# Attention and MLP on one core: PSUM banks named from group 6 on, and q and k of 28 blocks turned by transposing DMA

## The chip, the core and the metric

The kernel runs on one core of one Trainium2 chip. The metric is device time in microseconds (us). A profiled execution, taken by the hardware profiler, is read beside the times.

## The reference

```python
# 8 batches, 8 heads, 576 positions, 64 dimensions of a head; d_model 512, hidden 2048
scores = np.matmul(q, k.transpose(0, 1, 3, 2)) / np.sqrt(64)
rel = pos[:, None] - pos[None, :]
bias = slopes[:, None, None] * -np.abs(rel)          # slopes 2 ** -(h + 1)
scores = np.where((rel >= 0) & (rel < 128), scores + bias, -1e9)
attn = softmax(scores)
x = np.matmul(attn, v).transpose(0, 2, 1, 3).reshape(8, 576, 512)
xn = (x - mean) / np.sqrt(var + 1e-06) * g_ln
out = x + np.maximum(xn @ w_ch1, 0.0) @ w_ch2
```

A query sees itself and the 127 positions before it, so a block of 128 queries needs the keys of its own block and of the one before.

## The kernel before

**Blocks and groups.** The rows are cut into 36 blocks of 128. The batches go in four pairs p; a pair has nine blocks: four of each batch, in turn (`blk` 0, 2, 4, 6 of the first, 1, 3, 5, 7 of the second), and `blk` 8, called `T`, which holds the last 64 rows of both. The list `order` numbers them n = 0 to 35. The MLP works on groups of blocks: groups 0 to 5 have two blocks each (n = 0 to 11), groups 6 to 11 four each (group 6 is n = 12 to 15, group 11 is n = 32 to 35).

**Attention of a block.** q and k arrive with positions along partitions, and the scores need dimensions along partitions. `load_qk` (L213) loads q and k of both batches for 128 positions (index i = `blk // 2`; i = 4 is the tail) into a raw tile, from a pool of four buffers for each of q and k, cast to fp16 on the way by POOL's DMA. It puts two neighbouring positions side by side in a partition, so a piece of a transfer is two rows of 64 numbers. `turn` then does 64 TensorE transposes of 64x64 (L277) into two PSUM banks, and four copies (L296 for q, L297 for k; L302 for the tail), one bank's on VectorE (DVE), the other's on ScalarE (ACT). The queries come out with the even positions first and the odd ones behind; the mask `m_full`, made of exponentials of distances (`decay`, L118), has its columns in the same order, and stores of an output block go out as two DMAs, one of even and one of odd rows. `scores` (`attend`, L381) writes products into one of two score tiles of two PSUM banks each, and ScalarE takes their exponential (L389). `masks` multiplies with the decay on VectorE (L400). `values` multiplies with v, which `load_v` (L223) has loaded (L433), and divides by the sum (L441, L442).

**Layer norm.** `stats` takes mean and variance on VectorE (L530, L531), and two small POOL operations (L485, L488) make `rstd` of them. `normal` centres and scales a block into `xc` (L472) and issues a transposing DMA on SP's queue (L480) that puts it into `xT`, the input of the MLP. Blocks of the first groups are turned by TensorE in place of that.

**MLP.** `mlp1(g)` is the first layer: 16 units of four matmuls into one PSUM bank each (L665), and a ReLU (L681, mostly on ScalarE). For groups 0 to 5 `mlp2` is the second layer (L698) and `finish` (L809) adds x. For groups 6 to 11 `fast_mlp2` does the second layer with seven products of half blocks in place of eight, from sums and differences of quarters of the hidden tile (`combine_hidden`, L733, on VectorE) and of the weights (made once). The products are accumulated in four PSUM banks x, y, z and w, in the order x, y, z, x, z, x, w (L757); after each of them VectorE adds a bank to the output (`add`, L770), and `send` stores two blocks at a time.

**PSUM.** Four of the eight banks are the two score tiles. The others are the pool `ps_mm`, with one tag: each tile that is asked for takes the next of the four in turn, be it for a unit of the first layer, a product of the second, values or a turn. A turn uses the score tiles where its call has `in_sc`, as all those in the loop over the later blocks have.

**Order.** The order of instructions on TensorE, VectorE and ScalarE is written out by hand: `steps` is a list of the attention's steps, and `weave_at(units, places)` goes through the units of a layer and puts the next step behind each unit whose number is in `places`. From group 6 on there is one loop:

```python
for g in range(6, len(GROUPS)):
    weave_at(mlp1(g), 0, 2, 5, 7, 8, 10, 13, 15, also=(1, 4) if g == 6 else ())
    weave_at(fast_mlp2(g), 1, 3, 6, 7, 7, 9, 12, 13)
```

Each block n from 8 on has four steps: a turn of the keys and queries three blocks ahead (if there is one to do); values of n and scores of n + 2; masks of n + 1 and n + 2, and statistics of n; `normal`. Loads are issued on POOL by `load_until`, with each block's values, so far as the list of loads is due (`place`, `AHEAD`). The order on POOL and on SP (loads, small operations, stores, transposing DMAs) is the scheduler's.

Of the kernel before, what the change touches and what calls it, by code (L numbers as in the profile page):

```python
# [11 lines left out]
FP32 = mybir.dt.float32  # L12
# [5 lines left out]
P = 128  # L18
# [4 lines left out]
T = 8  # L23
# [15 lines left out]
def distances():  # L39

    key = np.arange(P)[:, None]
    query = np.arange(P)[None, :]

    def far(rel, ok=True):
        return np.where(ok & (rel >= 0) & (rel < WINDOW), rel, FAR)

    ends = [far(P + query - HALF * b - key, query // HALF == b) for b in range(2)]  # L50
    tail = far(query - key, query // HALF == key // HALF)
    evens_first = np.r_[0:P:2, 1:P:2]
    both = [far(P + query - key), far(query - key)]
    cols = [m[:, evens_first] for m in both] + [*ends, tail]
    return np.concatenate(cols, axis=1).astype(np.float16)
# [3 lines left out]
def kernel(  # L59
# [24 lines left out]
    consts = pool("consts", 1)  # L84
    raw_pool = pool("raw", 4)
    turned_pool = pool("turned", 3)
    probs_pool = pool("probs", 4)
# [13 lines left out]
    dist = consts.tile([P, 5 * P], FP16)  # L101
    nc.sync.dma_start(out=dist, in_=dist_dram.ap())
    iden = consts.tile([P, P], FP16)
# [9 lines left out]

    def decay(m, at):

        n = m.shape[2]
        for h in range(H):
            nc.scalar.activation(  # L118
                out=m[:, h, :],
                in_=dist[:, at * P : at * P + n],  # L120
                func=AF.Exp,
                scale=-(2.0 ** (-8.0 * (h + 1) / H)),
            )

    g_sb = consts.tile([P, NKB], FP32)
# [79 lines left out]
    raw = {}  # L205

    def load_qk(src, tag, p, i):

        n = min(P, S - i * P)
        t = raw_pool.tile([P, H, 2, D], FP16, tag=tag, name=tag)  # L210
        raw[tag, p, i] = t
        for b in range(2):
            nc.gpsimd.dma_start(  # L213
                out=t[b * n // 2 : (b + 1) * n // 2],
                in_=src[2 * p + b, :, i * P : i * P + n, :].rearrange(
                    "h (c r) d -> c h r d", r=2
                ),
            )
# [64 lines left out]
    def turn(p, i, in_sc=False, copies=(nc.vector.tensor_copy, nc.scalar.copy)):  # L283

        ps = [bank(b if in_sc else None) for b in range(2)]
        k = keys_tile("k", p, i)  # L290
        if i < 4:
            q = queries(p, i)
            transposed("q", p, i, [t[:, 0] for t in ps])
            transposed("k", p, i, [t[:, 1] for t in ps])
            for b, copy in enumerate(copies):
                copy(out=q[:, b], in_=ps[b][:, 0])  # L296
                copy(out=k[:, b].rearrange("p h (c r) -> p r h c", r=2), in_=ps[b][:, 1])  # L297
        else:
            q = keys_tile("q", p, i)
            for tag, t, dst, copy in zip("qk", ps, (q, k), copies):  # L300
                transposed(tag, p, i, [t[:, 0]])
                copy(out=dst[:, 0].rearrange("p h (c r) -> p r h c", r=2), in_=t[:, 0])  # L302

# [17 lines left out]
    def turn_first():  # L321
# [12 lines left out]
        nc.vector.tensor_copy(out=g_row, in_=ps_row)  # L334

    weights_of, unmasked, scored = {}, {}, []

# [3 lines left out]
    def seen(p, blk, o, t):  # L341


        both, every = slice(0, 2), slice(0, HALF)
        first, second = slice(0, HALF // 2), slice(HALF // 2, HALF)
        if p == 0 and blk < SEEN:
# [4 lines left out]
        if o == blk:  # L351
            return [(0, both, every), (1, both, second)]
        return [(1, both, every), (0, both, first)]

# [64 lines left out]
    def values(p, blk, hg):  # L419

        if hg == 0:
# [4 lines left out]
            if n < BY_DMA:  # L426
                sums[p, blk] = small.tile([P, 2], FP32, tag="sum", name="sum")
        ps = ps_mm.tile([P, 4, D + 1], FP32, tag="mm", name="ps_pv")
        terms = weights_of[p, blk]
# [189 lines left out]
    steps += [values_steps(5)[0], turn_step(6, True), values_steps(5)[1], scores_step(6)]  # L619
    steps += [x_step(5) + masks_of(6), scores_step(7) + variance_of(4), values_steps(6)[0]]  # L620

    steps += [values_steps(6)[1], x_step(6) + masks_of(7), variance_of(5)]
    steps += [*values_steps(7), x_step(7) + variance_of(6)]
    steps += [turn_step(8) + variance_of(7), scores_step(8) + turn_step(9)]
    steps += [[(scores_tail, 0)] + scores_step(9) + masks_of(8)]


    for n in range(8, count):
        first_half, second_half = values_steps(n)
        steps.append(  # L630
            turn_step(n + 3, True) if n + 3 < count and order[n + 3][1] % 2 == 0 else []
        )
# [23 lines left out]
    def mlp1(g, on_dve=()):  # L656
# [5 lines left out]
        for u, fb in enumerate(turn_about if g >= FAST else range(NFB)):  # L662
            ps = ps_mm.tile([P, 4 * P], FP32, tag="mm", name="ps_m1")
            for kb in range(NKB):
# [70 lines left out]
    def fast_mlp2(g):  # L735
# [13 lines left out]

        banks = {}  # L750

        def product(name, lhs, rhs, first):
            if first:
                banks[name] = ps_mm.tile([P, 2, QD], FP32, tag="mm", name="ps_f")
            for pair in range(pairs):
                for fb in range(QF):
                    nc.tensor.matmul(  # L757
                        banks[name][:, pair, :],
                        lhs[:, fb, pair * P : (pair + 1) * P],
                        rhs[:, fb, :],  # L760
                        start=(first and pair == 0 and fb == 0),
                        stop=(fb == QF - 1),
                        skip_group_check=True,
                    )
                yield DM

        def add(name, i, j, to_x):
            x, o = rows(i)
            cols = slice(j * QD, (j + 1) * QD)
            nc.vector.tensor_tensor(  # L770
                out=o[:, :, cols],
                in0=banks[name][:, 0:pairs, :],
                in1=(x if to_x else o)[:, :, cols],
                op=ALU.add,
            )

        def send(i):
            _, o = rows(i)
            for at in range(pairs):
                store(*members[g][i * pairs + at], o[:, at, :])  # L780

# [19 lines left out]
        add("x", 1, 1, False)  # L801
        yield from product("w", a[1][1], t4, True)
        add("w", 1, 0, False)
        send(1)

# [12 lines left out]

    def store(p, blk, o):
        for b, t0, w, p0 in spans(p, blk):  # L820
            dst, src = out[b, t0 : t0 + w, :], o[p0 : p0 + w, :]
            if blk == T:
                nc.sync.dma_start(out=dst, in_=src)
            else:
                dst = dst.rearrange("(c r) d -> r c d", r=2)
                for r in range(2):
                    nc.sync.dma_start(out=dst[r], in_=src[r * HALF : (r + 1) * HALF])

# [18 lines left out]
    with tc.manual_schedule(engines={engine.PE}):  # L847
        with tc.manual_schedule(engines={engine.Activation, engine.DVE}):
# [13 lines left out]
            weave_at(mlp1(5), 0, 1, 4, 8, 10, 12, also=(3, 6, 9))  # L862
            weave_at(mlp2(5), 0, 1, 2, 4, 6, 7)
            for g in range(6, len(GROUPS)):
                weave_at(
# [34 lines left out]
```

## Time and profile before

| what | value |
|---|---|
| median of three runs | 334.84 us (334.58 to 335.43) |
| profiled execution | 334.56 us, of which span 332.8 us |
| instructions | 10421 |
| matmuls of the first layer, L665 | 116.9 us in 640 |
| matmuls of the second layer, L698 and both groups of L757 | 46.0 in 192, 45.8 in 384, 22.5 in 192 |
| masks L400, adds L770 on VectorE | 688 ns and 684 ns each |
| statistics L530, scaling L472 on VectorE | 685 ns and 412 ns each |
| ReLU L681, exponentials of scores L389 on ScalarE | 497 ns and 1026 ns each |
| DMA packets | 101728, of them 92849 under 512 bytes |
| stores of 128 KB, SP's queue | 72, 2.4 us from issue to landing |
| loads of q, k, v of 128 KB, POOL's queue | 32 each, 5.2, 5.6 and 6.5 us from issue to landing |
| granted TensorE clock, by slices | 0.9 or more of full speed; 0.7 in slice 25 and 0.8 in the last |

An engine's busy time is the sum over its instructions; a matmul's weight load (PEld) overlaps with other matmuls and is counted for itself. A line number is that of the helper that issues an instruction, so the three products x, the two z, y and w all stand at L757, told apart by the tile that they read (`ht`, a quarter of the hidden tile, or `hs`, a sum of such). "Waits" lists what ended the idle time ahead of an instruction. The times of all DMA engines together are given as a share of 16 engines' span, or in a window as a mean busy share.

### The profile page before, as it was taken

To read this page: it belongs to the slowest core of one execution; us is meant where nothing else is said; L and a number is where in the kernel's file an instruction comes from. 1 tells how busy PE (TensorE), PEld (TensorE's weight loads), DVE (VectorE), ACT (ScalarE), POOL (GpSimd) and SP (SyncE) were. 2 spreads that over 40 slices of the span, in tenths; PEclk is the share of its full clock that TensorE was granted. 3 is DMA by queue.
4 is the path that set the end of the run, shared out by engine and by line. 5 is a ranking of instruction groups with operands and counts; after the bars stand their busy time and mean duration, and the time that the engine had idled before them with its cause. 6 is when DMAs were issued, how large, how long until landed. Compare 5 with 4: busy or idle time off the path is not lost.

```text
span 332.8 us, 10421 instructions
## 1 busy us (share of the span) xinstructions
PE 309.3 (93%) x4478; PEld 208.2 (63%) x4478; DVE 234.4 (70%) x555; ACT 184.6 (55%) x320; POOL 114.8 (35%) x188
## 2 busy tenths in 40 slices
PE   8889999998999999999799979999899979999992
PEld 3478556757567575558655866567656854685582
DVE  2879777786777887669775986589758975761462
ACT  6688666676656583684278533763287218405600
POOL 8933677666425652813252541300000000000000
PEclk9999999999999999999999997999999999999998
DMA  9999999999599696996396966351430033015005
GB/s 112 167 207 191 189 152 195 173 140 146 47 145 96 76 157 58 160 66 65 42 164 86 97 65 98 85 43 18 81 81 18 18 80 82 18 23 121 0 2 126
DMA packets 101728, 32.34 MB, mean 97 GB/s; under 512 B 92849, under 2 KB 97073, under 8 KB 101682
## 3 DMA queue, kind: packets, MB, share of 16 engines
q0 software_dynamic: 79872, 18.36, 64.9%
q1 hardware_dynamic: 21810, 13.32, 19.4%
q8 instruction: 35, 0.57, 0.8%
q14 instruction: 11, 0.09, 0.1%
HBM read 36.90 MB, written 9.44 MB: 139 GB/s over the span
## 4 chain that ended last, share of the span: by engine, by line
PE 71%; DVE 10%; ACT 7%; POOL 4%; DMA 4%; issue 2%; DVEq 0%; POOLq 0%; ACTq 0%
PE ps_m L665 31%; PE ps_f L757 21%; PE ps_m L698 9%; ACT probs L389 4%; DMA w<-in_moe_w_ch_dram 4%; PE ps_sc L381 4%; PE ps_pv L433 4%; PE ps_sc L277 2%; DVE probs L400 2%; DVE st L530 2%; POOL vx L223 1%; DVE o L770 1%; POOL q L213 1%; DVE k L297 1%; POOL rstd L488 1%
## 5 line engine op out<-in xcount | busy, mean ns | idle before, releaser
L665 PE MATMUL ps_m<-xT,w1g 128*128 128x512 f16 (+1 forms) x640 | 116.9, 337 | 1.1 <-ACT ht L681 0.8
L681 ACT ACTIVATE ht<-ps_m 128x512 f16<-128x512 f32 (+1 forms) x187 | 89.2, 497 | 39.6 <-PE ps_m L665 36.7
L665 PEld LDWEIGHTS <-w1g 128*128 128x128 f16 x640 | 60.1, 98 | 48.8 <-issue 1.8
L389 ACT ACTIVATE probs<-ps_sc 128x1024 f16<-128x1024 f32 x56 | 54.3, 1026 | 39.7 <-PE ps_sc L381 39.7
L757 PE MATMUL ps_f<-w,ht 128*128 128x256 f16 x384 | 45.8, 279 | 8.7 <-DVE o L770 8.7
L757 PEld LDWEIGHTS <-ht 128*128 128x128 f16 x384 | 37.9, 100 | 14.9 <-issue 9.4
L485 POOL TENSOR_TENSOR rstd<-moments,powers 128x1 f32<-128x1 f32 x28 | 5.4, 192 | 118.6 <-DVE moments L531 118.6
L698 PE MATMUL ps_m<-w,ht 128*128 128x512 f16 x192 | 46.0, 380 | 0.0
L223 POOL DMA_DIRECT2D vx<-in_v_dram x40 | 34.7, 880 | 26.7 <-PE ps_pv L433 12.5
L400 DVE TENSOR_TENSOR probs<-probs,m 128x1024 f16<-128x1024 f16 x56 | 37.4, 688 | 9.1 <-ACT probs L389 8.7
L213 POOL DMA_DIRECT2D q<-in_q_dram x40 | 27.3, 688 | 20.2 <-PE ps_sc L277 12.0
L442 DVE SCALAR_TENSOR_TENSOR x<-ps_pv,rec 128x256 f16<-128x256 f32 x72 | 30.6, 425 | 2.5
L213 POOL DMA_DIRECT2D k<-in_k_dram x40 | 26.9, 686 | 5.9 <-DMA w<-in_moe_w_ch_dram 3.6
L698 PEld LDWEIGHTS <-ht 128*128 128x128 f16 x192 | 17.1, 98 | 17.4
L472 DVE TENSOR_SCALAR xc<-x,moments,rstd 128x512 f16<-128x512 f16 x28 | 11.5, 412 | 19.9 <-POOL rstd L488 19.9
L530 DVE BATCH_NORM_STATS2 st<-x 128x6 f32<-128x512 f16 x36 | 24.6, 685 | 0.0
L296 ACT COPY q<-ps_sc 128x512 f16<-128x512 f16 x15 | 8.8, 586 | 28.0 <-PE ps_sc L277 27.8
L381 PE MATMUL ps_sc<-q,k 64*64 64x128 f16 (+1 forms) x1088 | 20.4, 208 | 3.8 <-ACT probs L389 1.1
L441 DVE RECIPROCAL rec<-ps_pv 128x4 f32<-128x4 f32 x72 | 12.7, 176 | 15.9 <-PE ps_pv L433 15.5
L757 PE MATMUL ps_f<-w,hs 128*128 128x256 f16 x192 | 22.5, 273 | 0.0
L770 DVE TENSOR_TENSOR o<-ps_f,x 128x512 f32<-128x512 f32 x24 | 16.4, 684 | 7.6 <-PE ps_f L757 7.5
L433 PEld LDWEIGHTS <-probs 128*128 128x128 f16 x448 | 18.7, 97 | 4.7 <-DVE probs L400 0.3
(79 smaller groups left out, 345.5 us busy)
## 6 DMA issues: line engine op xcount, KB each, us to landing
out_dram<-o SPq DMA_DIRECT2D x72, 128.0 KB, 2.4
q<-in_q_dram POOLq DMA_DIRECT2D x32, 128.0 KB, 5.2
k<-in_k_dram POOLq DMA_DIRECT2D x32, 128.0 KB, 5.6
vx<-in_v_dram POOLq DMA_DIRECT2D x32, 128.0 KB, 6.5
w<-in_moe_w_ch_dram POOLq DMA_DIRECT2D x8, 512.0 KB, 10.7
q<-in_q_dram POOLq DMA_DIRECT2D x8, 64.0 KB, 4.7
k<-in_k_dram POOLq DMA_DIRECT2D x8, 64.0 KB, 4.5
vx<-in_v_dram POOLq DMA_DIRECT2D x8, 64.0 KB, 5.9
```

What stands on the lines that cost most here:

```text
L213: nc.gpsimd.dma_start(out=t[b * n // 2 : (b + 1) * n // 2], in_=src[2 * p + b, :, i * P : i * P + n, :].rearrange("h (c r) d -> c h r d", ...
L223: nc.gpsimd.dma_start(out=vx[p0 : p0 + n, :, 0:D], in_=v[b, :, t0 : t0 + n, :].rearrange("h p d -> p h d"),)
L381: nc.tensor.matmul(in_halves(ps[cols, j, n, t, :])[:, r, queries], kt[rows, hp, cols], in_halves(qt[rows, b, hp])[:, r, queries], start=Tr ...
L389: nc.scalar.activation(out=dst.rearrange("p (n j) q -> p j n q", j=2), in_=ps.rearrange("p j n t q -> p j n (t q)"), func=AF.Exp, scale=in ...
L400: nc.vector.tensor_tensor(out=dst, in0=dst, in1=mask, op=ALU.mult)
L433: nc.tensor.matmul(ps[:, i, :], pr[:, h, t, :], vext[(p * NSLOT + o) % NV][:, h, :], start=(n == 0), stop=(n == len(terms) - 1),)
L442: nc.vector.scalar_tensor_tensor(out=xs[p, blk][:, hg * 4 * D : (hg + 1) * 4 * D].rearrange("p (h d) -> p h d", h=4), in0=ps[:, :, 0:D], s ...
L530: nc.vector.bn_stats(out=st, in_=xs[order[n]])
L665: nc.tensor.matmul(ps[:, 0:cols], w[:, kb, fb * P : (fb + 1) * P], xT[:, kb, 0:cols], start=(kb == 0), stop=(kb == NKB - 1),)
L681: nc.scalar.activation(out=ht[:, fb, 0:cols], in_=ps[:, 0:cols], func=AF.Relu)
L698: nc.tensor.matmul(sums[at], ht[:, fb, at * P : (at + 1) * P], w2[:, fb, :], start=(fb == 0), stop=(fb == NFB - 1),)
L757: nc.tensor.matmul(banks[name][:, pair, :], lhs[:, fb, pair * P : (pair + 1) * P], rhs[:, fb, :], start=(first and pair == 0 and fb == 0), ...
```

## The change

It has these parts:

- **Loads and turns.** `by_dma(p, i)` is true for all of the pairs 1 to 3 and for the tail of pair 0: blocks 8 to 35. For these, `load_qk` loads positions in natural order, one row of 64 numbers as a piece, and `turn` issues transposing DMAs on SP, two for each of q and k (one for a tail), in place of TensorE's transposes and the copies. A turn issued in this way needs no PSUM. The raw pool goes from four buffers to three, the pool of turned tiles from three to four.
- **Order of queries.** Blocks 8 on have their queries in natural order. `m_full` is computed again in that order once block 7's masks have been made: `in_order` loads the distances anew on SP, and eight exponentials follow on ScalarE in two halves. The range of queries that a key half can see, in `seen`, is then a contiguous half. Rows of these blocks are stored with one DMA, not two.
- **Places.** The turns of blocks 8 and 9 (the tail's tile, and the first of pair 1) are called some steps earlier; that of block 11 is called at n = 8, and the later ones four blocks ahead, not three.
- **Banks.** From group 6 on, the four banks of `ps_mm` are four fixed tiles in a list `ring`. `psum()` takes the first of the list and puts it at its end, for the first layer's units and for values. `fast_mlp2` takes the first for x, the second for y and for z too, and the third for w, and leaves the third and fourth to others meanwhile; afterwards the list is put in a new order.
- **Last group.** There w has a bank for each pair of blocks, so that one block's w is added (256 columns of one block) while the other's runs; the second half of the columns is stored ahead of that, and stores alternate between SP's and ScalarE's queue.

```diff
-    cols = [m[:, evens_first] for m in both] + [*ends, tail]
+    cols = [m[:, evens_first] for m in both] + [*ends, tail] + both
...
-    raw_pool = pool("raw", 4)
-    turned_pool = pool("turned", 3)
+    raw_pool = pool("raw", 3)
+    turned_pool = pool("turned", 4)
...
+    def in_order():
+        nc.sync.dma_start(
+            out=dist[:, 0 : 2 * P], in_=dist_dram.ap()[:, 5 * P : 7 * P]
+        )
...
+    def by_dma(p, i):
+        return p > 0 or i == 4
...
+        if by_dma(p, i):
+            t = raw[tag, p, i] = t.rearrange("p h r d -> p (h r d)").rearrange(
+                "p (b h d) -> p b h d", b=2, h=H
+            )
         for b in range(2):
+            if by_dma(p, i):
+                dst = t[:, b] if i < 4 else t[b * n : (b + 1) * n, 0]
+                nc.gpsimd.dma_start(
+                    out=dst,
+                    in_=src[2 * p + b, :, i * P : i * P + n, :].rearrange(
+                        "h p d -> p h d"
+                    ),
+                )
+                continue
...
+        k = keys_tile("k", p, i)
+        if by_dma(p, i):
+            q = keys_tile("q", p, i)
+            for tag, dst in (("q", q), ("k", k)):
+                src = raw.pop((tag, p, i))
+                for b in range(2 if i < 4 else 1):
+                    nc.sync.dma_start_transpose(
+                        out=dst[:, b], in_=src[:, b].rearrange("p h d -> p (h d)")
+                    )
+            return
...
+    ring = []
+    def psum(name, banks=None):
+        if not ring:
+            return ps_mm.tile([P, DM], FP32, tag="mm", name=name)
+        t = (banks or ring)[0]
+        if banks is None:
+            ring.append(ring.pop(0))
+        return t
...
-            return [(0, both, every), (1, both, second)]
-        return [(1, both, every), (0, both, first)]
+            return [(0, both, every), (1, slice(1, 2), every)]
+        return [(1, both, every), (0, slice(0, 1), every)]
...
-    steps += [turn_step(8) + variance_of(7), scores_step(8) + turn_step(9)]
+    steps += [values_steps(6)[1], x_step(6) + masks_of(7) + [(in_order,)], variance_of(5)]
+    steps += [
+        values_steps(7)[0] + turn_step(9),
+        [(decay, m_full, 0, low)] + values_steps(7)[1],
+        x_step(7) + variance_of(6),
+    ]
+    steps += [[(decay, m_full, 0, high)] + variance_of(7), scores_step(8)]
...
-            turn_step(n + 3, True) if n + 3 < count and order[n + 3][1] % 2 == 0 else []
+            [f for m in ahead  # [n + 4], and [11] at n = 8
+             if m < count and order[m][1] % 2 == 0 for f in turn_step(m)]
...
-        banks = {}
+        x_bank, y_bank, *others = ring
+        use = dict(x=[x_bank] * 2, y=[y_bank] * 2, z=[y_bank] * 2, w=others[:1] * 2)
+        if g == len(GROUPS) - 1:
+            use["w"] = others
+        ring[:] = others
...
-        yield from product("w", a[1][1], t4, True)
-        add("w", 1, 0, False)
-        send(1)
+        if use["w"][0] is use["w"][1]:
+            ring[:] = [others[1], y_bank, x_bank, others[0]]
+            yield from product("w", a[1][1], t4, True)
+            add("w", 1, 0, False)
+            send(1)
+        else:
+            low, high = slice(0, QD), slice(QD, DM)
+            send(1, cols=high, queues=(nc.sync, nc.scalar))
+            for at, _ in enumerate(product("w", a[1][1], t4, True)):
+                add("w", 1, 0, False, slice(at, at + 1))
+                send(1, [at], low, (nc.sync, nc.scalar))
+                yield DM
...
+            if by_dma(p, blk // 2):
+                next(queues).dma_start(out=dst, in_=src)
...
+            ring += [ps_mm.tile([P, DM], FP32, tag="mm", name="ps_r") for _ in range(4)]
             for g in range(6, len(GROUPS)):
```

## The prediction

> **What bounds the kernel now.** I read the page first, then the list of who waited for whom on TensorE, then the timeline, one stretch per stage. The page's shares and the chain that ended last:
>
> ```profile
> PE 309.3 (93%) x4478; PEld 208.2 (63%) x4478; DVE 234.4 (70%) x555; ACT 184.6 (55%) x320; POOL 114.8 (35%) x188
> ...
> q0 software_dynamic: 79872, 18.36, 64.9%
> q1 hardware_dynamic: 21810, 13.32, 19.4%
> ...
> PE 71%; DVE 10%; ACT 7%; POOL 4%; DMA 4%; issue 2%; DVEq 0%; POOLq 0%; ACTq 0%
> ```
>
> TensorE carries the span, so an instruction taken off its queue is worth its issue time, and a wait put into it costs its length. Waits there are few (line waited for: total us, times, longest):
>
> ```profile
> PE ps_f L757 <- DVE o L770: 8.7, 4, 2.2
> ...
> PE ps_sc L277 <- DMA k<-in_k_dram: 1.0, 2, 0.5
> PE ps_sc L381 <- DVE k L297: 0.9, 2, 0.7
> ...
> PE ps_sc L381 <- ACT k L297: 0.3, 2, 0.2
> ```
>
> The largest, 8.7 us, comes once in each of groups 6 to 9. Their second layer (`fast_mlp2`) is the product sequence x, y, z, x, z, x, w; here is group 8 (start us, us, engine, line):
>
> ```profile
> 221.69 3.67 PE L757 MATMUL ps_f<-w,ht 128*128 128x256 f16 x32
> ...
> 225.20 2.78 PE L757 MATMUL ps_f<-w,hs 128*128 128x256 f16 x24
> ...
> 226.09 0.55 POOL L488 TENSOR_TENSOR rstd<-rstd,powers 128x1 f32<-128x1 f32 x1
> ...
> 226.97 0.41 DVE L472 TENSOR_SCALAR xc<-x,moments,rstd 128x512 f16<-128x512 f16 x1
> 227.29 0.68 DVE L770 TENSOR_TENSOR o<-ps_f,o 128x512 f32<-128x512 f32 x1
> ...
> 227.91 0.45 PE L277 MATMUL ps_sc<-iden,q 64*64 64x64 f16 x32
> ...
> 228.55 1.05 PE L757 MATMUL ps_f<-w,hs 128*128 128x256 f16 x8
> ...
> 233.81 0.66 DVE L770 TENSOR_TENSOR o<-ps_f,x 128x512 f32<-128x512 f32 x1
> ...
> 234.52 3.65 PE L757 MATMUL ps_f<-w,ht 128*128 128x256 f16 x32 [2.11 <-DVE o L770]
> ...
> 239.07 5.35 PE L665 MATMUL ps_m<-xT,w1g 128*128 128x512 f16 x24
> ...
> 239.56 0.68 DVE L770 TENSOR_TENSOR o<-ps_f,o 128x512 f32<-128x512 f32 x1
> ```
>
> Line 1 is x and y, line 2 z and half of the second x, 227.91 a turn of q and k, 234.52 the third x and w. The third x waits for the add of the second x (233.81), which stands on VectorE behind two masks and the statistics of a block. The add of y ends at 227.97, 2.8 us after y ended at 225.20; nobody waits for it, since z has a bank of its own. VectorE ran without a gap from 221.2 to then.
>
> **The change, part by part.** Sums are made against the profiled execution: 334.56 us, 332.8 of it span. The median of the three runs is 0.28 higher.
>
> *Turns off TensorE.* From the turn's start to the next matmul is 0.64 us at 227.91 and in every full turn, 0.62 in the half turns of i = 4. Twelve full and four half turns go: 12 x 0.64 + 4 x 0.62 = 10.2 us, half of it (5.1) before group 6 starts at 135.3, half behind. VectorE and ScalarE lose 28 copies each, about 17 and 19 us. With the copies go the waits for k in the list above, 0.9 + 0.3, and one of the two for a k load (0.5; the other is at the start, which stays): 1.7, all early but for the 0.2 us that scores behind a turn wait in the later groups (229.79 to 229.98 in group 8), 0.6 over four.
>
> *Mask again.* `m_full` is computed anew: 8 exponentials of 0.41 us (row L118, 128x256) = 3.3 us of ScalarE near 59 to 65 us, half of it between Relus that come every 0.44 us and take 0.39. The copies it loses there come later, so I charge 0.5 of the 1.6 us (bounds 0 and 1.6). Early sum: -5.1 - 1.7 + 0.5 = -6.3.
>
> *z in y's bank.* The order of instructions and their waits in the changed kernel show the first matmul of z waiting for the add of y, and VectorE's order between is unchanged: statistics, add of x, a combination, xc, add of y. No copy of a turn stood in that stretch, so nothing makes it faster. The price is the end of that add + 0.05 us (as 234.47 to 234.52) less the end of y: group 6 2.6, 7 2.6, 8 2.8, 9 2.7, 10 2.0 (293.91 against 291.98), 11 0.9 (318.90 against 318.02). Sum 13.6. The wait of the third x stays: `add("x", 0, 1)` stands behind the same masks.
>
> *POOL's order.* In the new order a load of q or k stands between the two small operations that make rstd, for blocks 8, 12, 14, 16, 19, 21 and 23 among others; before they always follow at once (225.82 and 226.09). Blocks 19 and 23 matter: their xc stands right before the add of y in groups 6 and 7. Block 19's load waits until a transposing DMA has emptied its raw buffer; those (three in SP's queue, 1.19 us each) wait for scores that end at 152.0, so the third is issued at 154.4 and lands by 157.0 (2.6); the load takes 0.9, rstd 0.6, and xc starts at 158.5, not 157.0. Block 23: 192.4, not 191.1. The stall grows by 1.5 + 1.3 = 2.8. Bounds: 0, if the transposes are earlier, and 5.
>
> *The other banks.* The second unit of the next first layer takes w's bank, and waits for the add at 239.56 to 240.24; it would start at 239.07 + 0.86. That is 0.35 in each of groups 6 to 9, 1.4.
>
> *SP and the loads.* 56 transposes of 1.19 us add 67 us to SP's queue; store issues fall from 72 to 49 on SP and 2 on ACT. xT of block 27, the last of group 9, is issued at 227.4, lands by 230, and is needed at 239.07: 9 us of cover. The 64 loads concerned move twice the packets, 128 bytes each as v's: 0.88 us to issue in place of 0.69, 6.5 us to land in place of 5.2. Loads run 20 to 40 us ahead (k for the turn at 118 left at 75), so I take 0. If that cover went, scores would wait for load, issue and transpose, up to 10 us once.
>
> By the Trainium skill (DMA: Bandwidth & Descriptors, Specifications) transfers under 512 B miss line rate, a rule against this part; 92849 of the page's 101728 packets are already below that, and by the rule loads would come later still, which is the DMA rival below.
>
> *The tail.* Today the last add ends at 327.65, four stores are issued 0.6 us apart, and 3.3 us after the last issue the span ends. Afterwards the last add has half the columns (0.4 us), and one store each on two queues follows: 0.3 + 1.7 = 2.0 saved.
>
> Sum: -6.3 - 5.1 - 0.6 + 13.6 + 2.8 + 1.4 - 2.0 = +3.8, which gives **338.4 us**.
>
> **Rivals.**
> *VectorE comes in time (faster).* If the add of y came on average 2.1 us after y rather than 2.7 (16.4 over six groups), the sum would be zero; at 1.5 it is -3.6 and the time 331, with no stall at all 322. For it: VectorE is 17 us lighter. Against: none of that lies in the stretch.
> *The clock.* After its 2.24 us wait, group 7 ran at half clock for 3.4 us:
>
> ```profile
> 198.92 5.32 PE L757 MATMUL ps_f<-w,ht 128*128 128x256 f16 x32 [2.24 <-DVE o L770]
> ...
> 199.40:202.80 3.40, 3.40 (x21) 2.50 (x19) 1.92 (x4) 0.00 (x0) 0.00 (x0) 0.56 0.37 75
> ```
>
> 32 matmuls took 5.32 us in place of 3.65: 1.7 lost. Waits of 2.11, 2.14 and 2.20 did not trigger it. Now there are five waits of 2 to 4 us more. My sum keeps one such event; three more make 343.5. The Trainium skill (TensorE: Matmul & The Clock Gate, Why this matters for your kernels) puts the limit at gaps of about 3 us, so by it only groups 6 and 7 would add events and the sum be 341.8; the trace's 2.24 is below that limit.
> *DMA becomes the bound.* 28672 more packets (48 loads of 512, 16 of 256) at today's mean (64.9% of 332.8 us over 79872) are 78 us of the engines, and 56 transposes at most 2.3 each (all of q1's share over 28) 129: 85% of the span becomes 147%. But shares overlap: the windows view has 2.18 at 60 to 70 us without a wait. If loads run late, one 10 us wait makes 348.
>
> **Numbers.** A measurement of this kernel tells about 0.3%, 1.0 us, from no change. Forecast (336 to 341) 0.45; clock 0.15 and DMA 0.07, both slower; faster by VectorE 0.2; near balance of the terms, within 0.3%, 0.13. Slower 0.67. The range takes the early and POOL bounds and the clock: 332 to 344.5.
>
> **What would show it.** Right: z's first matmul waits for the add of y, 2 to 4 us, six times; no turn before scores of block 8 on; the 2.1 us waits of the third x remain; groups 6 to 9 take longer, the time up to 135 shrinks by 6. Wrong: z starts within 1 us of y's end, scores wait for a transpose, or the first layer waits for xT.

## The result: 402.7 us in place of 334.7, a ratio of 1.193 (1.180 to 1.207)

The changed kernel takes 402.68 us in the median (397.11 to 404.67), the kernel before 334.71 us beside it. The forecast was 338.4 us and its range ended at 344.5. The ratio is that of the two faster of the four executions, 397.1 and 400.8 us; the other two, the profiled one among them, lie more than 1.5% above the fastest and are left out of it. The profiled execution took 404.52 us, its span is 402.7. Lines have moved: L713 is the first layer (L665 before), L811 and L828 the products and adds of `fast_mlp2` (L757, L770), L229 the load of q and k in natural order, L318 the transposing DMAs of a turn, L509 and L517 `normal` (L472, L480), L522 and L525 rstd (L485, L488), L876 the add in `finish`.

The page of the changed kernel: busy time per engine, two queues, and the shares of the chain that ended last:

```profile
PE 322.8 (80%) x3582; PEld 210.0 (52%) x3582; DVE 220.1 (55%) x528; ACT 172.1 (43%) x300; POOL 125.8 (31%) x188
...
q0 software_dynamic: 108544, 18.36, 66.2%
q1 hardware_dynamic: 52178, 20.60, 28.0%
...
PE 38%; DMA 28%; DVE 13%; POOL 10%; issue 6%; ACT 2%; SPq 1%; POOLq 0%; DVEq 0%; ACTq 0%
```

TensorE has 896 instructions fewer and is busy 13.5 us longer; its mean granted clock is 0.907 of full speed, where it was 0.990 before. It held 71% of the chain before; now it holds 38%, and DMA and POOL together hold as much. So the kernel has another bound in part of its time. Who waits for whom tells which (line waited for: total us, times, longest); first TensorE's waits, then, from the list for all engines, three that were 19.9 us, nothing and nothing before:

```profile
PE ps_r L811 <- DVE o L828: 28.5, 10, 6.1
PE ps_pv L470 <- DVE ht L721: 13.9, 1, 13.9
PE ps_m L713 <- DVE x L479: 7.8, 2, 5.5
PE ps_m L713 <- DVE o L876: 6.7, 3, 3.6
```

```profile
DVE xc L509 <- POOL rstd L525: 77.7, 24, 19.0
...
POOL k L229 <- DMA k<-k: 38.0, 9, 6.7
...
POOL q L229 <- DMA q<-q: 27.9, 10, 6.5
```

TensorE waits for VectorE, VectorE's `xc` waits for POOL's rstd, and POOL's loads of q and k wait for transposing DMAs (`k<-k`, `q<-q`) that have yet to empty a raw buffer. The longest of these waits, in the timeline of all engines (start us, us, engine, line; idle time and its end in brackets):

```profile
82.09 0.18 DVE L568 BATCH_NORM_AGGREGATE moments<-st 128x2 f32<-128x6 f32 x1
...
84.95 1.85 POOL L229 DMA_DIRECT2D q<-in_q_dram  x2 [1.88 <-DMA q<-q]
...
89.30 0.87 POOL L246 DMA_DIRECT2D vx<-in_v_dram  x1 [2.50 <-DMA k<-in_k_dram]
...
93.52 0.87 POOL L229 DMA_DIRECT2D q<-in_q_dram  x1 [0.82 <-DMA q<-q]
...
99.01 0.20 POOL L522 TENSOR_TENSOR rstd<-moments,powers 128x1 f32<-128x1 f32 x1
99.67 0.93 POOL L229 DMA_DIRECT2D q<-in_q_dram  x1 [0.46 <-DMA vx<-in_v_dram]
100.62 0.58 POOL L525 TENSOR_TENSOR rstd<-rstd,powers 128x1 f32<-128x1 f32 x1
...
101.23 0.41 DVE L509 TENSOR_SCALAR xc<-x,moments,rstd 128x512 f16<-128x512 f16 x1 [18.96 <-POOL rstd L525]
101.56 1.08 DVE L721 TENSOR_SCALAR ht<-ps_m 128x256 f16<-128x256 f32 x3
101.67 1.19 SPq L517 DMA_TRANSPOSE xT<-xc  x1
...
102.03 0.38 PE L470 MATMUL ps_pv<-vx,own 128*128 128x65 f16 x4 [13.93 <-DVE ht L721]
```

The moments are there at 82.27. rstd is two operations of 0.2 and 0.6 us, but ten loads stand ahead of it on POOL and are issued first. Of the 16.7 us to 99.01, issuing these loads takes 8.5, waits for transposing DMAs that empty a raw buffer 2.7, and waits that the profile puts down to earlier loads landing 4.5. `xc` starts 19 us late; behind it on VectorE stand three ReLUs, and TensorE needs the bank that one of them empties. Behind `xc` on SP stand xT and the next transposing DMAs, and for these POOL's next loads wait: a loop. From 110 us on, the chain that ended last runs round it, here for one round and the start of the next (start us, us, what):

```profile
153.47 6.86 DMA k<-k
...
160.89 1.76 POOL k L229 x2
...
162.94 0.57 POOL rstd L525
...
163.54 0.41 DVE xc L509
...
164.63 0.42 DVE x L479
...
165.71 0.82 PE ps_pv L470 x22
...
166.62 3.39 DMA q<-q
...
170.92 0.87 POOL q L229
...
172.87 0.57 POOL rstd L525
...
173.48 0.06 DVE xc L509
```

A transposing DMA frees the buffer of a load, rstd follows the load, `xc` follows rstd, a division on VectorE (L479) and TensorE follow `xc`, and behind them the next transposing DMA is issued.

By stretches, between the first matmuls of the groups' first layers:

| stretch | before, us | after, us | difference | forecast |
|---|---|---|---|---|
| up to group 6 | 135.29 | 169.49 | +34.2 | -6.3 |
| group 6 | 34.10 | 52.25 | +18.2 | +3.0 |
| group 7 | 35.73 | 43.53 | +7.8 | +2.8 |
| group 8 | 33.95 | 38.59 | +4.6 | +1.7 |
| group 9 | 34.03 | 37.26 | +3.2 | +1.6 |
| group 10 | 27.62 | 30.01 | +2.4 | +2.0 |
| group 11, to the last matmul's end | 26.20 | 27.15 | +1.0 | +0.9 |
| from there to the end | 5.87 | 4.47 | -1.4 | -2.0 |

The forecast of a group is its z and POOL terms and, in groups 6 to 9, 0.35 for the second unit, less two turns (1.28) and 0.15. It holds from group 10 on. The miss is ahead of it: 40.5 us up to group 6, 15 in group 6, 5 in group 7, and 3 and 2 in groups 8 and 9. For these two, the timeline of the changed kernel in group 8 answers to the one shown of before, and the windows view has the clock of the wait of the third x and of what follows (stretch, its length, busy time and instructions of PE, PEld, DVE, ACT and POOL, then granted clock, DMA share, GB/s):

```profile
281.45 3.67 PE L811 MATMUL ps_r<-w,ht 128*128 128x256 f16 x32
285.49 0.69 DVE L828 TENSOR_TENSOR o<-ps_r,x 128x512 f32<-128x512 f32 x1
287.02 0.69 DVE L828 TENSOR_TENSOR o<-ps_r,o 128x512 f32<-128x512 f32 x1
287.75 5.17 PE L811 MATMUL ps_r<-w,hs 128*128 128x256 f16 x32 [2.63 <-DVE o L828]
```

```profile
295.50:297.60 2.10, 0.01 (x1) 0.00 (x0) 2.05 (x4) 0.00 (x0) 0.42 (x2) 1.00 0.02 2
297.60:301.00 3.40, 3.35 (x17) 2.37 (x17) 1.01 (x2) 0.00 (x0) 0.32 (x1) 0.52 0.28 69
```

z waits 2.63 us for the add of y (2.8 forecast), and then 32 matmuls take 5.17 us in place of 3.65; the third x waits as before, and its 32 take 5.32. In the second line the clock is 0.52 for the 3.4 us behind the wait; before, only group 7 had such a stretch.

### The profile page after: what moved, and what is told of

Read it like the earlier page. It is cut to its first block, busy times and chain, and to the rows that moved or that the text cites. A ratio compares the mean times of both kernels' runs of the same rounds, so it can differ in the third digit from the quotient of the medians.

```text
span 402.7 us, 8710 instructions
## 1 busy us (share of the span) xinstructions
PE 322.8 (80%) x3582; PEld 210.0 (52%) x3582; DVE 220.1 (55%) x528; ACT 172.1 (43%) x300; POOL 125.8 (31%) x188
## 3 DMA queue, kind: packets, MB, share of 16 engines
q0 software_dynamic: 108544, 18.36, 66.2%
q1 hardware_dynamic: 52178, 20.60, 28.0%
## 4 chain that ended last, share of the span: by engine, by line
PE 38%; DMA 28%; DVE 13%; POOL 10%; issue 6%; ACT 2%; SPq 1%; POOLq 0%; DVEq 0%; ACTq 0%
PE ps_r L811 16%; PE ps_r L713 15%; DMA vx<-in_v_dram 7%; DMA q<-q 6%; DMA w<-in_moe_w_ch_dram 4%; DMA k<-k 4%; DMA q<-in_q_dram 4%; DMA k<-in_k_dram 4%; PE ps_m L713 3%; ACT probs L426 2%; DVE o L828 2%; POOL q L229 2%; DVE x L479 2%; DVE probs L437 2%; POOL k L229 2%
## 5 line engine op out<-in xcount | busy, mean ns | idle before, releaser
L713 PEld LDWEIGHTS <-w1g 128*128 128x128 f16 x640 | 64.5, 104 | 80.1 <-issue 24.5
L713 PE MATMUL ps_r<-xT,w1g 128*128 128x512 f16 x384 | 90.1, 393 | 9.1 <-DVE o L876 3.2
L729 ACT ACTIVATE ht<-ps_r 128x512 f16<-128x512 f32 x96 | 56.6, 598 | 47.9 <-PE ps_r L713 47.9
L811 PE MATMUL ps_r<-w,ht 128*128 128x256 f16 x384 | 50.6, 297 | 8.7 <-DVE o L828 8.7
L509 DVE TENSOR_SCALAR xc<-x,moments,rstd 128x512 f16<-128x512 f16 x28 | 11.6, 413 | 78.7 <-POOL rstd L525 77.7
L811 PEld LDWEIGHTS <-ht 128*128 128x128 f16 x384 | 40.6, 107 | 17.3 <-issue 9.4
L713 PE MATMUL ps_m<-xT,w1g 128*128 128x256 f16 x256 | 36.9, 304 | 15.3 <-DVE x L479 7.8
L729 ACT ACTIVATE ht<-ps_m 128x256 f16<-128x256 f32 x91 | 34.1, 385 | 25.3 <-PE ps_m L713 22.8
L811 PE MATMUL ps_r<-w,hs 128*128 128x256 f16 x192 | 28.1, 317 | 19.8 <-DVE o L828 19.8
L229 POOL DMA_DIRECT2D k<-in_k_dram x32 | 26.9, 844 | 48.7 <-DMA k<-k 38.0
L229 POOL DMA_DIRECT2D q<-in_q_dram x32 | 27.1, 849 | 36.7 <-DMA q<-q 27.9
L811 PEld LDWEIGHTS <-hs 128*128 128x128 f16 x192 | 21.7, 113 | 26.1 <-issue 20.9
L522 POOL TENSOR_TENSOR rstd<-moments,powers 128x1 f32<-128x1 f32 x28 | 5.6, 200 | 95.0 <-DVE moments L568 94.8
L828 DVE TENSOR_TENSOR o<-ps_r,x 128x512 f32<-128x512 f32 x24 | 16.4, 684 | 25.1 <-PE ps_r L811 25.1
L746 PEld LDWEIGHTS <-ht 128*128 128x128 f16 x192 | 17.8, 99 | 19.1 <-issue 1.1
(78 smaller groups left out, 334.7 us busy)
```

The source lines that it names most:

```text
L229: nc.gpsimd.dma_start(out=dst, in_=src[2 * p + b, :, i * P : i * P + n, :].rearrange("h p d -> p h d"),)
L713: nc.tensor.matmul(ps[:, 0:cols], w[:, kb, fb * P : (fb + 1) * P], xT[:, kb, 0:cols], start=(kb == 0), stop=(kb == NKB - 1),)
L729: nc.scalar.activation(out=ht[:, fb, 0:cols], in_=ps[:, 0:cols], func=AF.Relu)
L746: nc.tensor.matmul(sums[at], ht[:, fb, at * P : (at + 1) * P], w2[:, fb, :], start=(fb == 0), stop=(fb == NFB - 1),)
L811: nc.tensor.matmul(banks[name][pair][:, pair, :], lhs[:, fb, pair * P : (pair + 1) * P], rhs[:, fb, :], start=(first and fb == 0 and (pair ...
L828: nc.vector.tensor_tensor(out=o[:, at, cols], in0=banks[name][at.start][:, at, :], in1=(x if to_x else o)[:, at, cols], op=ALU.add,)
```

## Experiments

Times of the kernel before beside them were 334.0 to 335.0 us. Intervals are those of the ratio to it.

### The two halves of the change, each alone

```diff
 # kernel before, with ring, psum(), the new fast_mlp2 and store; load_qk, turn, m_full as before
+            ring += [ps_mm.tile([P, DM], FP32, tag="mm", name="ps_r") for _ in range(4)]
```

> The kernel before with the banks of the changed kernel alone (ring, z in y's bank, w's banks and the split last group), q and k turned by TensorE as before. Theory A (POOL's queue holds rstd behind loads that wait for transposing DMAs; the banks cost only their own waits): six waits of z for the add of y, 2.0 to 2.8 us each and 0.9 in the last group, 13.6 us in all, 1.4 us of the second unit's bank, 2.0 us saved at the end: 347.6 us; if the half clock after these waits shows here as it did in groups 8 and 9 of the changed kernel, 1.5 to 1.7 us more at each of up to seven of them, 354 to 358 us. Rival B (the banks carry the whole loss, the transposing DMAs are hidden): above 385 us.

351.9 us (349.1 to 355.7), ratio 1.049 (1.041 to 1.057). Its waits on TensorE:

```profile
PE ps_r L775 <- DVE o L792: 21.7, 10, 2.7
```

Of the ten, z has six (2.41, 2.52, 2.73, 2.62, 1.88, 0.78: 12.9 us), the third x four (8.7). TensorE is busy 313.8 us in place of 309.3 with as many instructions. In its trace the granted clock is half for three stretches of 3.4 us (from 15.5, 169.1 and 281.7), where the kernel before has one; two more cost 3.4 us, at 1.7 each, and the first of the three lies ahead of every named bank. From the last matmul's end to the span's end it takes 5.08 us in place of 5.87. 12.9 + 0.9 (second units) + 3.4 - 0.8 (the end) = 16.4 of the 17.4 that the span grew. The banks cost what the forecast said, and a clock.

```diff
 # changed kernel, with fast_mlp2 of the kernel before
-            ring += [ps_mm.tile([P, DM], FP32, tag="mm", name="ps_r") for _ in range(4)]
```

> The changed kernel with the banks, the second layer and the end of the kernel before: transposing DMAs, natural order and the earlier places remain. Theory A: the part before group 6 loses its 34 us as in the changed kernel, groups 6 and 7 lose some 15 us more from late xc, groups 8 to 11 run as before or 1.3 us each quicker: 375 to 385 us. Rival B (the banks carry the loss): within 5 us of 335 us.

379.2 us (374.7 to 380.1), ratio 1.131 (1.121 to 1.140). Group 6 begins at 169.40, as in the whole change. `xc` waits 82.6 us for rstd. So the larger part, 45 us, comes with the turns, and all of the loss up to group 6.

### Is it POOL, or the DMA engines?

```diff
 # changed kernel
-        nc.gpsimd.tensor_tensor(out=here, in0=moments[:, n, 1:2], in1=powers[:, 0:1], op=ALU.add)
-        nc.gpsimd.tensor_tensor(out=here, in0=here, in1=powers[:, 1:2], op=ALU.pow)
+        inv_std(n, 1)
```

> The changed kernel with rstd of blocks 8 to 35 made by nine small VectorE operations per block (those that the earlier blocks use) in place of two on POOL; POOL is left with loads. Theory A: the 77.7 us that xc waited for rstd go, VectorE carries some 1 us more per block; the loss of the early part shrinks from 34 us to under 10, the stalls of z return to 2.6 to 2.8 us plus the new operations in the stretch: 360 to 370 us. Rival C (the DMA engines are the bound: loads with twice the packets and 56 transposes land late and everything waits for them): the waits move from rstd to scores and values, above 390 us.

391.4 us (389.9 to 392.0). The time lies where the rival put it, above 390, but not for the rival's reason alone. The early part did nearly as theory A said: group 6 begins at 146.14, 10.9 us late and not 34.2, with SP's instructions in the order of the changed kernel but for one store. But VectorE is busy 40.2 us longer, 1.4 us for each of 28 blocks where I had put 1, and these operations stand ahead of the add of y: z waits up to 5.3 us. And the first layer now waited 8.6 us for xT once, while loads of q and k took 9.7 and 10.7 us to land (7.4 and 6.4 in the changed kernel). The edit moved the work to the engine that the next wait is on, so its time doesn't decide; where group 6 begins says that some 23 of the 34 us came with rstd on POOL.

```diff
 # kernel before, load_qk for blocks 8 to 35
+                    out=flat[0:n, b],
+                    in_=src[2 * p + b, :, i * P : i * P + n, :].rearrange("h p d -> p h d"),
```

> The kernel before, but q and k of blocks 8 to 35 loaded in natural order in pieces of 128 bytes, as in the changed kernel; they are still turned by TensorE as if they lay in pairs, so the rows of q and k are not those that the scores mean: only the time counts. 64 loads have twice the packets, no transposing DMA is added. Theory A: loads issue in 0.88 us and land some 1 to 2 us later, nothing on TensorE waits for them: within 1.5 us of 334.8 us. Rival C (packets saturate the DMA engines): loads land 10 us and more late in the part up to 135 us: above 345 us.

334.0 us, ratio 1.000 (0.997 to 1.004). 28672 packets more cost nothing: q0's share goes from 64.9% to 76.0%, and the loads of q and k land as fast as before (5.1 and 5.5 us).

```diff
 # changed kernel's turns with the banks of before; POOL by program order
-    with tc.manual_schedule(engines={engine.PE}):
+    with tc.manual_schedule(engines={engine.PE, engine.Pool}):
```

> The kernel with transposing DMAs and the banks of before (as in the run of the turns alone, 379.2 us), but POOL's order is that of the program: the two rstd operations of a block follow its loads at once, and no load stands ahead of or between them that the program calls for later. Theory A1 (the loss is the loop over POOL's queue: a load waits for a transposing DMA, rstd behind it, xc behind rstd, and xT and further transposing DMAs behind xc on SP): most of the 44 us go, 338 to 352 us, with the waits of xc for rstd down from 82.6 us to under 30. Theory C (the loads, the transposing DMAs and xT share DMA engines that are full from 40 to 130 us, and each lands late whatever the order): 365 us or more.

334.7 us (323.9 to 340.5 over ten executions, nine of them above 331), 335.0 for the kernel before: the 45 us are gone with one word. The word changes SP's order too, which stays the scheduler's: 19 transposing DMAs of turns stood ahead of the first xT in the run of the turns alone, 14 stand there now. What the two orders are worth apart from each other was not run. POOL in this run, at the place shown above:

```profile
84.78 0.18 POOL L522 TENSOR_TENSOR rstd<-moments,powers 128x1 f32<-128x1 f32 x1 [2.11 <-DVE moments L568]
85.05 0.56 POOL L525 TENSOR_TENSOR rstd<-rstd,powers 128x1 f32<-128x1 f32 x1
85.57 0.97 POOL L246 DMA_DIRECT2D vx<-in_v_dram  x1
```

POOL waits for the moments, and not the moments for POOL; `xc` waits 18.0 us for rstd in all. What remains is one wait of the first layer for xT (total, times, longest):

```profile
PE ps_m L713 <- DMA xT<-xc: 11.8, 2, 10.6
```

That xT's `xc` was ready at 91.2; xT was issued at 93.5, behind four transposing DMAs of a turn on SP (85.3 to 93.4), and took 8.2 us to land, where the second xT of the kernel before took 4.8 (the median of all there is 2.6). Group 6 begins at 141.42.

```diff
 # small pieces as in the run above, and beside each turn of blocks 8 to 35
+            for at in range(4 if i < 4 else 2):
+                nc.sync.dma_start_transpose(out=spare[at % 2], in_=m_tail[:, 0:4].rearrange(...))
```

> The kernel before with the DMA traffic of the changed kernel and none of its dependences: q and k of blocks 8 to 35 in pieces of 128 bytes, turned by TensorE as if they lay in pairs (rows of q and k are not those that the scores mean), and beside each of these turns four transposing DMAs (two at a tail) of 128x512 on SP, of a constant into a spare tile that nobody reads. Theory A1: SP's queue is longer by 56 x 1.2 us and xT lands some 1 to 2 us later with 9 us of cover: 334 to 339 us. Theory C: xT, loads and stores land late from 60 to 130 us: above 350 us.

402.1 us, and no test of either theory. With a constant as their source the transposing DMAs depended on nothing, and the scheduler put 32 of them in one row on SP, from 39.13 on:

```profile
39.13 71.93 SPq L272 DMA_TRANSPOSE spare<-m_tail  x32
```

Stores stood behind them, an add of `finish` waited for an output buffer, and TensorE for that, 50.2 us. It shows what a queue's order can cost (32 at 2.25 us each), but not the price of the traffic in its place.

### z's bank, and the wait that was there before

```diff
 # kernel before with named banks
-        use = dict(x=[x_bank] * 2, y=[y_bank] * 2, z=[y_bank] * 2, w=others[:1] * 2)
+        use = dict(x=[x_bank] * 2, y=[y_bank] * 2, z=[z_bank] * 2, w=[y_bank] * 2)
```

> The kernel before with the named banks and the split last group (as in the run of the banks alone, 351.9 us), but z has a bank of its own and w takes y's bank, which has been free since the add of y. Theory: the six waits of z (12.9 us there) go, and with them most of the half clock behind z; the waits of the third x (2.1 to 2.2 us in groups 6 to 9) remain as before, 1.5 us are saved at the end: 332 to 335 us. Rival (named banks as such cost, by the order in which units and values take them): above 340 us.

336.2 us, ratio 1.004 (1.000 to 1.007). z's waits are gone and the four of the third x (8.6 us) are there. So z's place in y's bank made 15.7 us, and named banks as such little; 336.2 lies a little above what I expected. The second units still wait 0.9 us, the end gives 0.8 and not 1.5, and TensorE is busy 312.7 us, 3.4 more than before: three stretches of half clock in place of one, the first from 14.5, ahead of every named bank.

```diff
 # kernel before
-                weave_at(fast_mlp2(g), 1, 3, 6, 7, 7, 9, 12, 13)
+                weave_at(fast_mlp2(g), 1, 3, 6, 7, 8, 9, 12, 13)
```

> The kernel before with one number changed: the masks and statistics that follow the second product x in the second layer of groups 6 to 11 are put one unit later, behind the first half of the second z, so that the add of the second x stands ahead of them on VectorE. Theory: the four waits of the third x (8.7 us) go, and the half clock of group 7 (1.7 us): 324 to 327 us. Rival (the add is late for another reason, or the masks then hold up the next values): 331 us or more.

325.8 us, ratio 0.973 (0.968 to 0.979). The four waits are gone, and group 7's half clock with them: the add of the second x now stands ahead of the masks.

### Do the parts add up?

```diff
 # changed kernel, whole
-    with tc.manual_schedule(engines={engine.PE}):
+    with tc.manual_schedule(engines={engine.PE, engine.Pool}):
```

> The changed kernel whole, with POOL's order that of the program, as in the run where that took the turns alone from 379.2 to 334.7 us. Theory A1 (POOL's order carries the loss of the turns, the banks theirs, and the two add up): 334.7 + 17.9 = 353 us, with waits of z for the add of y of 12 to 14 us, 348 to 358. Rival (the z stalls in groups 6 and 7 were long for another reason than rstd held up by a load, or late xT adds to the stalls): above 362 us.

353.3 us, ratio 1.058 (1.049 to 1.066), with z waiting 13.8 us. The same edit on the kernel before is the control:

> Control: the kernel before with POOL's order that of the program, nothing else. Theory A1: its raw buffers are emptied by TensorE's transposes, so no load is held up for long and the order matters little: 333 to 337 us. Rival (an order by hand is better whatever turns the blocks, and that is what the other run gained): 325 us or less.

334.5 us, ratio 0.999 (0.995 to 1.003). An order by hand gains nothing where TensorE empties the raw buffers. The medians, us:

| turns of the 28 blocks | banks of before | banks of the change |
|---|---|---|
| TensorE | 334.7 | 351.9 |
| transposing DMA, POOL as scheduled | 379.2 | 402.7 |
| transposing DMA, POOL in program order | 334.7 | 353.3 |

The columns differ by 17 to 24 us, and the two last rows by 45 and 49.

```diff
 # changed kernel
-    raw_pool = pool("raw", 3)
-    turned_pool = pool("turned", 4)
+    raw_pool = pool("raw", 4)
+    turned_pool = pool("turned", 3)
```

> The changed kernel with the two pool sizes of before (raw 4, turned 3), nothing else. Theory A1 says that a load on POOL is held up until a transposing DMA has emptied its raw buffer; a fourth buffer frees it one turn earlier: between 353 us, where POOL's order cost nothing, and 385 us. Rival (POOL's order alone matters, the loads wait as long with four, or the scheduler moves them that much farther ahead): 395 us or more.

395.6 us (393.0 to 397.1), `xc` waits 74.8 us. The two sizes together give back 7 us, less than the 18 and more that I expected, and the time is the rival's. So most of the loss stays with one raw buffer more and one turned tile fewer; a fourth raw buffer beside four turned tiles was not run.

### A version that beats both

```diff
 # kernel before, masks later; in the last group, as in the changed kernel:
-        yield from product("w", a[1][1], t4, True)
-        add("w", 1, 0, False)
-        send(1)
+            send(1, cols=high, queues=(nc.sync, nc.scalar))
+            for at, _ in enumerate(product("w", a[1][1], t4, True)):
+                add("w", 1, 0, False, slice(at, at + 1))
+                send(1, [at], low, (nc.sync, nc.scalar))
```

> The kernel before with the masks one unit later (325.8 us by itself) and the last group's w in two banks with split stores, turns on TensorE. The split end saved 1.5 us in the span of the changed kernel (5.9 us from the last matmul's end to the span's end before, 4.4 us after): 324.3 us, between 323.5 and 325.5.

325.2 us, ratio 0.972 (0.964 to 0.980). The split end is worth 0.8 us here (5.87 us from the last matmul's end before, 5.10 now). The changed kernel's 1.4 had a second source: with the turns alone, whose rows go out in one store, the end is 5.39.

```diff
 # the kernel with turns by transposing DMA, banks of before and POOL in program order; that last group, and
-                weave_at(fast_mlp2(g), 1, 3, 6, 7, 7, 9, 12, 13)
+                weave_at(fast_mlp2(g), 1, 3, 6, 7, 8, 9, 12, 13)
```

> Transposing DMAs with POOL's order that of the program (334.7 us, 323.9 to 340.5 over ten executions), the masks one unit later, and the split end; banks as before. The waits of the third x (8.6 us in that run's profile) and the half clock after three of them (4.9 us) go, and 1.5 us at the end: 334.7 - 15.0 = 319.7 us, between 313 and 326 us, with a wait of the first layer for xT of some 10 us still in it in most executions. Rival (DMA landings become later as the rest gets faster): 325 us or more.

321.3 us (319.1 to 321.7), ratio 0.960 (0.952 to 0.967): the fastest. Its page, and its one long wait on TensorE:

```profile
PE 297.4 (93%) x3582; PEld 199.5 (62%) x3582; DVE 219.6 (69%) x528; ACT 171.6 (54%) x300; POOL 126.1 (39%) x188
```

```profile
PE ps_m L713 <- DMA xT<-xc: 9.6, 1, 9.6
```

```diff
 # the same, load_qk of blocks 8 to 35 but for the tails
-                    out=dst,
-                    in_=src[2 * p + b, :, i * P : i * P + n, :].rearrange("h p d -> p h d"),
+                out=pairs[b * n // 2 : (b + 1) * n // 2],
+                in_=src[2 * p + b, :, i * P : i * P + n, :].rearrange("h (c r) d -> c h r d", r=2),
```

> The kernel with transposing DMAs, POOL's order that of the program, masks later and split end (321.3 us), but q and k of the blocks 8 to 35 other than the tails loaded in pieces of 256 bytes again, two positions side by side, and transposed as they lie: the rows of q and k are not those that the scores mean, only the time counts. If the first layer's one wait for xT (9.6 us near 100 us) comes from loads in small pieces that share the DMA engines with xT: the wait shrinks to under 4 us, 314 to 317 us. If it comes from the transposing DMAs themselves, ahead of xT in SP's queue and on the same engines: 319 to 322 us.

320.5 us, but from 315.2 to 329.1: two of the four executions (315.2 and 316.1) lie in the range for the small pieces, two above both ranges (324.8 and 329.1), and the profiled one (329.1) still waits 7.2 us for xT. It doesn't tell small pieces from transposing DMAs; the cause of that wait beyond the 2.3 us in SP's queue stays open.

## Why the prediction was wrong

**The step that failed is "POOL's order".** It named the mechanism (a load between or ahead of the rstd operations waits for a transposing DMA) and the right engines, and put 2.8 us on it, bounds 0 and 5. The orders on POOL and SP together cost 45 us with the banks of before and 49 with the new ones. Two things were wrong in the working. It priced two blocks, 19 and 23, whose `xc` stands right before an add of y, and put nothing on the others (8, 12, 14, 16, 21); but behind the late ones stand ReLUs, divisions and adds that TensorE waits for. In group 7 the `xc` right before the add of y waited 1.31 us for rstd, as forecast (1.3), but the two ahead of it 3.99 and 3.09, and z waited 6.02 us. And it took one delay for itself, from a time table in which the transposing DMAs are issued when the scores end; in fact their place on SP is behind xT, and xT's is behind `xc`, so each delay is the cause of the next. From 82.3 to 99.0 one rstd waited 16.7 us; there the loads ahead of it cost more by their number (8.5 us to issue ten) than by their waits for transposing DMAs (2.7).

**The early part** was to shrink by 6.3 and grew by 34.2. Even with POOL in program order it grows by 5.3 (whole change) to 6.1 us: a wait of 10 us for xT of group 4 outweighs what the turns bring. This is a second step that failed, "SP and the loads", a term put at 0: "9 us of cover" was read off group 9, and used for all groups. One wait of 10 us was the price of the DMA rival (0.07), for scores; here it is xT that came late. With POOL in program order the whole change still takes 353.3 us, 15 above the forecast; the wait for xT (9.9) and five stretches of half clock in groups 6 to 9 beyond the one that the sum kept (an estimate of 8.5, at 1.7 each) are enough for that.

**z in y's bank**: 13.6 forecast, 12.9 measured by itself; 19.8 in the changed kernel, where in groups 6 and 7 late `xc` made it 6.06 and 6.02 (16.4 forecast with POOL's term). Right but for that term. The second units cost 0.9 (1.4 forecast), the end gives 1.4 (2.0), of which the split w makes 0.8, and the third x waited on as said.

**The clock** was a rival at 0.15 (three more events) and came true beside the rest. Half clock followed waits of 2.6 to 3.0 us and of 2.14, each time for some 3.4 us. In the run with POOL in program order three of four waits of 2.14 to 2.19 us brought it; the one at 169.0 of 2.14 did not, nor did 2.52 to 2.73 in the run of the banks alone. So no length of a wait decides. The Trainium skill (TensorE: Matmul & The Clock Gate, What's actually happening) says that the monitor looks through free-running windows of about 3.4 us. The traces agree: past its start, all stretches of half clock of a trace begin whole multiples of 3.41 us apart (in the changed kernel 287.47, 297.71 and 335.25: 3 and 11). This grid can be laid over each of the 16 traces. From 40 us on, full clock turned to half behind 65 of its windows, in which TensorE had idled 1.90 us or more (by the profile, where matmul ends are modelled); behind 1246 others, with 1.95 or less, it stayed full. So about 1.9 us of idle time inside one window decides, and a wait that the grid cuts in two can pass: the wait that ended at 169.0 has 0.40 us in one window and 1.74 in the next, the one of 2.73 has 1.44 and 1.29, while the one of 2.19 has 2.04 in the first. The gap of about 3 us that the prediction quotes from that page of the Trainium skill gave groups 8 and 9 no half clock; in the changed kernel both had it.

**Turns off TensorE** do bring time: from group 6 to the end, 193.6 us against 197.5 with POOL in program order, though three third x ran at half clock there and one before.

**The rivals.** VectorE in time fell: with the turns' copies off VectorE and POOL in program order z's waits are 13.8 us, so its lighter load did not reach the stretch. DMA as the bound: small pieces cost nothing, and the fastest version moves the packets of the changed kernel (108544 and 52178 on the two queues) in 321.3 us. Landing times did get longer beside the transposing DMAs: loads of q, k and v issued from 60 to 80 us land after 12.7 us in the median in the changed kernel, 5.7 before and 5.4 with small pieces alone. But with POOL in program order they take 13.8, and the 45 us are gone all the same. There the landing times show as one wait of 10 us, for an xT (the first four of which the trace has the landing take 6.2 to 8.5 us in that run and in the fastest, 4.4 to 4.8 before).

## What to carry to other kernels

When a copy moves from a compute engine to a queue, list for each in-order queue what stands behind the instructions that now wait for it, and follow the chain until it either ends or comes back to the same queue; if it comes back, the price is a loop's, not one wait's. A tiny operation on a queue that issues loads (rstd here) belongs ahead of any load that can be held up for a buffer, and an order that a scheduler made is to be written out by hand there. A cover that was read in a quiet stretch must be read again in the busiest one.

## What the runs showed of the hardware that was not expected

- Twice the packets for q and k, 128 bytes each, made no difference to the time (ratio 1.000, 0.997 to 1.004), although the engines' share of q0 rose from 64.9% to 76.0%.
- A transposing DMA of 128x512 from SP lands after 2.4 us at the least; in the changed kernel those of the turns took 4.1 to 4.4 us in the median and 11.3 at the longest.
- Beside such transposing DMAs, loads from POOL took twice as long to land (12.7 us in the median of those issued from 60 to 80 us, 5.7 before).
- A wait of TensorE of 2.14 us can halve its clock for 3.4 us (32 matmuls in 5.3 us, not 3.65), and one of 2.73 can pass without. What counted in the 16 traces was about 1.9 us of idle time inside one window of a fixed grid of 3.41 us (65 windows with 1.90 us or more, against 1246 with 1.95 or less).
